# Biases on GpSimd, evenly cut q and k work, spread v and w_out loads, and an odd PV distance in a fused attention and feed-forward kernel

## The chip, the cores and the metric

The kernel runs on one core of one Trainium2 chip. The metric is the device time of one execution in microseconds (us), taken on that core. Executions of one kernel mostly lie within about 1% of each other, and chips differ a little; so every kernel was run beside the kernel before on the same chip, and ratios are taken against those runs. An execution is called slow if it lies over 1.5% above the fastest of its kernel, and slow ones are left out of ratios.

## The reference

Thresholded attention over 8 batches of 8 heads (576 rows, head size 64), followed by a feed-forward block over all 4,608 rows (512 to 2,048, leaky ReLU, back to 512).

```python
scores = scale * np.matmul(q, k.transpose(0, 1, 3, 2))
thresh = np.max(scores, axis=-1, keepdims=True) - tau
scores = np.where(scores >= thresh, scores, -1000000000.0)
scores = scores - np.max(scores, axis=-1, keepdims=True)
attn = np.exp(scores)
attn = attn / (np.sum(attn, axis=-1, keepdims=True) + 1e-09)
x = np.matmul(attn, v)            # heads are then laid side by side
h = x @ w_in
out = np.maximum(0.01 * h, h) @ w_out
```

## The kernel before

The program is a hand-ordered software pipeline of 144 steps. A step takes one block of 128 query rows for two heads, and a batch has 18 steps. In the first two batches PV takes one block at a time, later mostly two. In the text, "step 43" is the pass of the loop below with s = 43. Engines run their own instructions in exactly this order. The feed-forward block is worked off beside it in units: an h unit makes a piece of the hidden layer (hp, then gT), an o unit a part of the output (op, then osb).

```python
# one pass of the step loop (cut)
scores(s, sc)                                   # TensorE: sc = q k^T, three fp16 products
sa, sB = smax(0, sc, mx), smax(1, sc, mx)       # VectorE: sf = C * sc, and its row maximum; the two "sf"
bb = sb.tile([128, 2], FP32, tag="bb", ...)
nc.vector.tensor_scalar(out=bb, in0=mx, scalar1=-1.0, scalar2=tau_f, op0=AX.mult, op1=AX.add)
nc.scalar.activation(out=P_[:, 1, :], in_=sB, func=AF.Identity, bias=bb[:, 1:2], scale=1.0)
nc.gpsimd.tensor_scalar(out=P_[:, 0, :], in0=sa, scalar1=1.0, scalar2=bb[:, 0:1], ...)   # from step 4 on
leak()                                          # VectorE: gT = 0.01 * hp + gT
for f in (h, o): ...                            # ScalarE: gT = relu; VectorE: osb = op (output copy)
evacs = [pv(ui) for ui in pv_at.get(s, [])]     # TensorE: P V, LAG steps after its scores
if now is not None:
    nc.vector.reciprocal(out=rc, in_=usm[now])  # 1 / row sum
    nc.vector.tensor_scalar(out=W_[..., 1152:1280], in0=rc (broadcast), ...)             # "w copy"
    nc.sync.dma_start(out=uwt[now], in_=W_, transpose=True)                              # wt
# the clamp: int16 max on the bits of fp16
anchor[0] = nc.vector.tensor_scalar(out=pi, in0=pi, scalar1=NEG, scalar2=None, op0=AX.max)
for h in range(2):
    nc.scalar.activation(out=uW[ui][:, i, ds(576*h, 576)], in_=P_[:, h, :], func=AF.Exp, accum_out=...)
for f in evacs: f()                             # VectorE: xT = pv * (1 / row sum)
for t in ptick.get(s, []): t()                  # GpSimd: q and k work, ordered behind the clamp
for t in tick.get(s, []): t()                   # loads, transposes, ScalarE casts
```

The work for the next batch is hung on the steps of this one. q and k are loaded, split into an fp16 high and low part (ScalarE casts `hi`; GpSimd scales, `x64`, and subtracts, `lo`) and transposed by DMA (`turn`) into `kst` and `qst`:

```python
for b in range(1, B):
    s0 = 18 * (b - 1)
    for hb in range(2):
        t0 = s0 + PREP + (5 if b >= NARROW else 3) * hb       # PREP = 6
        if b == 1:
            t0 += 2
        at(t0 - 4, lambda b=b, hb=hb: load_half(k, kms, "km", b, hb))    # SyncE's queue, 576 KB
        at(t0 - 3, lambda b=b, hb=hb: load_half(q, qms, "qm", b, hb))
        at(t0 - 1, lambda b=b, hb=hb: hi("k", b, hb))
        at(t0 + 2, lambda b=b, hb=hb: hi("q", b, hb))
        ...                                                   # x64, lo and turn, six steps
    for i in range(4):
        at(max(s0 + 10, 12) + i, lambda b=b, i=i: load_v(b, i))          # GpSimd's queue
for g in range(8):
    at(WOUT + g // 2, lambda g=g: load_w_out(g))              # WOUT = 1: two of 256 KB in a step
```

## Time and profile before

| | us |
|---|---|
| Device time, first three runs | 546.72 median (546.09 to 549.38) |
| Span of the profiled run | 546.5 |
| Start, up to step 43 | 170.0 |
| Steps 43 to 133 (five batches of 18 steps) | 300.2, 60.0 per batch |
| Steps 133 to 143 | 33.4 |
| Tail after step 143 | 42.9 |

A step is counted from its R, the start of VectorE's second accumulator read in it, as in the prediction below.

Busy time by stretch, for the middle and for steps 6 to 12 (columns: stretch, us, then busy us and instructions of TensorE, its weight loads, VectorE, ScalarE and GpSimd, granted clock, that is the share of TensorE's full clock that it was given, DMA share, GB/s):

```profile
170.03:470.24 300.21, 277.79 (x2916) 171.38 (x2914) 293.75 (x823) 255.42 (x566) 160.93 (x209) 0.99 1.10 204
35.30:59.36 24.06, 18.01 (x183) 11.35 (x182) 16.45 (x56) 16.56 (x38) 10.86 (x14) 0.59 1.09 244
```

VectorE is busy 293.75 of 300.21 us in the middle, and the DMA share is 1.10 (over 1, so the records of packets overlap). Both look full. The waits of the middle (columns: us in total, times, longest us) seem to settle it for VectorE:

```profile
PE pv L367 <- DMA wt<-w: 1.6, 2, 1.3
DVE sf L396 <- PE sc L336: 1.5, 3, 0.8
```

TensorE waited for a transposed wt for 1.6 us in five batches, and VectorE for scores for 1.5. Nobody waits for a transfer worth speaking of.

### The profile page before, as it was taken

How to read it: one execution, taken by the hardware profiler on the slowest of the kernel's cores; microseconds unless marked ns; L12 is line 12 of the kernel's file. 1: busy time of each engine (PE TensorE's matmuls, PEld its weight loads, DVE VectorE, ACT ScalarE, POOL GpSimd, SP SyncE). 2: the span in 40 equal slices, each digit the busy share in tenths (PEclk: the TensorE clock that was granted, in tenths of full speed). 3: DMA queues.
4: the chain of work that ended last, by engine and by line, in shares of the span. 5: the costliest groups of instructions: out<-in, count | busy, mean ns of one | idle time of the engine just before them, and what ended most of it. 6: DMA issues, size and time to landing. Idle time of an engine off the chain costs nothing. (4 is left out here: it accounts for less than half of the span.)

```text
span 546.5 us, 14352 instructions
## 1 busy us (share of the span) xinstructions
PE 484.4 (89%) x5328; PEld 305.0 (56%) x5328; DVE 491.3 (90%) x1385; ACT 423.4 (77%) x922; POOL 253.2 (46%) x338
## 2 busy tenths in 40 slices
PE   5558987989999888988989899999999899999996
PEld 4325654656666555555555555555565565666663
DVE  5766997999999999999999999999999999999542
ACT  5657875888888888898788888898888888888430
POOL 5344761268425772468325852477335842222000
PEclk9655998999999989999999999999999999999999
DMA  8999999999999999999999999999999999667401
GB/s 215 192 161 288 163 169 175 203 222 199 181 184 208 241 191 164 217 242 180 189 197 256 194 174 175 234 239 190 188 219 247 203 195 182 129 134 125 109 24 58
DMA packets 280133, 101.85 MB, mean 186 GB/s; under 512 B 254976, under 2 KB 267264, under 8 KB 280064
## 3 DMA queue, kind: packets, MB, share of 16 engines
q1 hardware_dynamic: 267008, 92.03, 87.4%
q0 software_dynamic: 13056, 8.92, 12.8%
q8 instruction: 41, 0.67, 0.5%
q14 instruction: 28, 0.23, 0.2%
HBM read 36.70 MB, written 9.44 MB: 84 GB/s over the span
## 5 line engine op out<-in xcount | busy, mean ns | idle before, releaser
L559 ACT ACTIVATE w<-P 128x576 f16<-128x576 f16 x288 | 193.9, 674 | 34.5 <-DVE P L554 25.5
L396 DVE TENSOR_SCALAR_CACHE_REDUCE sf<-sc 128x576 f32<-128x576 f32 x288 | 204.7, 746 | 11.0 <-PE sc L336 10.9
L525 POOL TENSOR_SCALAR P<-sf,bb 128x576 f16<-128x576 f32 x140 | 107.8, 770 | 196.9 <-DVE bb L523 179.6
L336 PE MATMUL sc<-kst,qst 64*128 64x320 f16 (+1 forms) x1536 | 142.2, 298 | 30.5 <-DVE sf L396 23.7
L241 PE MATMUL hp<-xT,win 128*128 128x128 f16 (+1 forms) x1600 | 153.8, 244 | 2.9 <-DVE xT L377 2.7
L241 PE MATMUL op<-wout,gT 128*128 128x512 f16 x576 | 149.1, 382 | 7.8 <-DVE osb L277 4.6
L524 ACT ACTIVATE P<-sf,bb 128x576 f16<-128x576 f32 x144 | 111.2, 772 | 56.3 <-DVE bb L523 53.5
L241 PEld LDWEIGHTS <-win 128*128 128x128 f16 x1600 | 124.0, 99 | 45.1 <-issue 7.9
L336 PEld LDWEIGHTS <-qst 64*128 64x128 f16 x1536 | 77.6, 97 | 81.0 <-issue 54.3
L223 DVE SCALAR_TENSOR_TENSOR gT<-hp,gT 128x512 f16<-128x512 f32 x144 | 98.4, 683 | 12.7 <-ACT gT L255 12.7
L255 ACT ACTIVATE gT<-hp 128x512 f16<-128x512 f32 x144 | 83.3, 579 | 19.0 <-PE hp L241 19.0
L241 PEld LDWEIGHTS <-gT 128*128 128x128 f16 x576 | 46.6, 98 | 70.4 <-issue 25.1
L554 DVE TENSOR_SCALAR P<-P 128x1152 int16<-128x1152 int16 x144 | 82.9, 576 | 0.0
L367 PE MATMUL pv<-wt,v 128*64 128x256 f16 (+2 forms) x1160 | 59.1, 240 | 8.0 <-DMA wt<-w 7.3
L367 PEld LDWEIGHTS <-v 128*64 128x64 f16 x1160 | 40.4, 112 | 25.4 <-issue 14.5
L559 ACT ACTIVATION_READ_ACCUMULATOR w<-P 128x1 f32 x288 | 53.8, 187 | 0.0
L159 POOL TENSOR_TENSOR ks<-km,ks 128x320 f16<-128x320 f32 (+1 forms) x56 | 40.8, 748 | 6.0 <-DVE P L554 4.8
L159 POOL TENSOR_TENSOR qs<-qm,qs 128x576 f16<-128x576 f32 x28 | 35.8, 1278 | 16.5 <-DVE P L554 12.7
L544 DVE TENSOR_SCALAR w<-rc 128x256 f16<-128x256 f32 (+1 forms) x92 | 36.5, 396 | 3.2
L523 DVE TENSOR_SCALAR bb<-mx 128x2 f32<-128x2 f32 x144 | 34.2, 238 | 5.0
L377 DVE TENSOR_TENSOR xT<-pv,wt 128x128 f16<-128x128 f32 x128 | 33.3, 292 | 2.5 <-PE pv L367 2.4
L277 DVE COPY osb<-op 128x512 f32<-128x512 f32 x36 | 24.5, 680 | 4.1 <-PE op L241 4.1
(33 smaller groups left out, 210.3 us busy)
## 6 DMA issues: line engine op xcount, KB each, us to landing
km<-in_k_dram SPq DMA_DIRECT2D x16, 576.0 KB, 4.8
qm<-in_q_dram SPq DMA_DIRECT2D x16, 576.0 KB, 5.0
out_dram<-osb SPq DMA_DIRECT2D x36, 256.0 KB, 3.8
v<-in_v_dram POOLq DMA_DIRECT2D x16, 160.0 KB, 5.0
v<-in_v_dram POOLq DMA_DIRECT2D x16, 128.0 KB, 5.0
win<-in_moe_w_in_dram POOLq DMA_DIRECT2D x8, 256.0 KB, 9.6
wout<-in_moe_w_out_dram POOLq DMA_DIRECT2D x8, 256.0 KB, 9.1
wt<-w SPq DMA_TRANSPOSE x92, 5.6
```

The lines of the kernel that those rows point to most:

```text
L159: return nc.gpsimd.tensor_tensor(out=dst[:, h], in0=src[:, h], in1=h_[:, h], op=AX.subtract)
L223: nc.vector.scalar_tensor_tensor(out=G.g[u], in0=hp, scalar=0.01, in1=G.g[u], op0=AX.mult, op1=AX.add)
L241: nc.tensor.matmul(out=out_, lhsT=lhsT, rhs=rhs, start=start, stop=stop, skip_group_check=True)
L255: nc.scalar.activation(out=G.g[u], in_=hp, func=AF.Relu, bias=0.0, scale=0.99)
L336: nc.tensor.matmul(out=sc[h][:, cols], lhsT=qt[r, g, qi, ds(2 * c, 2), :].rearrange("p t r -> p (t r)"), rhs=rhs, start=(i == 0), stop=(i ...
L367: nc.tensor.matmul(out=o_[ds(64 * h, 64)], lhsT=vt[:, pp, h, j, :], rhs=w_[:, :, 4 * h + j, :], start=(j == 0), stop=(j == 4), skip_group_ ...
L396: nc.vector.tensor_scalar(out=sf, in0=sc[h][:, ds(SC0, 576)], scalar1=C, scalar2=None, op0=AX.mult, op1=AX.max, accum_out=mx[:, h : h + 1])
L524: nc.scalar.activation(out=P_[:, 1, :], in_=sB, func=AF.Identity, bias=bb[:, 1:2], scale=1.0)
L525: (nc.vector if s < SPOOL else nc.gpsimd).tensor_scalar(out=P_[:, 0, :], in0=sa, scalar1=1.0, scalar2=bb[:, 0:1], op0=AX.mult, op1=AX.add)
L544: nc.vector.tensor_scalar(out=W_[:, :, 1152:1280].rearrange("p i (h r) -> p i h r", h=2), in0=rc[:, 0:nw, :].unsqueeze(3).to_broadcast([12 ...
L554: anchor[0] = nc.vector.tensor_scalar(out=pi, in0=pi, scalar1=NEG, scalar2=None, op0=AX.max)
L559: nc.scalar.activation(out=uW[ui][:, i, ds(576 * h, 576)], in_=P_[:, h, :], func=AF.Exp, bias=exp_bias, scale=1.0, accum_out=usm[ui][:, i, ...
```

## The change

The intent is to relieve VectorE: the two-column bias bb goes to GpSimd. PV runs seven steps behind its scores instead of six (an odd distance), so that the two xT evictions leave the steps that hold rc and w. GpSimd's q and k work is cut into seven even pieces in place of uneven ones over six steps, begins earlier, and no longer shares steps with the loads of v, which move to the steps after a batch's start. The w_out loads go one to a step over eight steps instead of two to a step over four. In the tail every second output copy goes to ScalarE, and the o units' endings are placed before the h units'.

```diff
-    LAG = 6
+    LAG = 7
-    PREP = 6
+    PREP = (4, 10)
+    PREP1 = (5, 10)
-    OSB_ACT = False
+    LAGN = 6
-    WOUT = 1
+    WOUT = 2
@@ osb_act
-        return OSB_ACT
+        osbs[0] += 1
+        return tail[0] and osbs[0] % 2 == 0
@@ q and k work
-            t0 = s0 + PREP + (5 if b >= NARROW else 3) * hb
-            if b == 1:
-                t0 += 2
+            t0 = s0 + (PREP1 if b < 2 else PREP)[hb]
             at(t0 - 4, ... load_half(k, kms, "km", b, hb))
             at(t0 - 3, ... load_half(q, qms, "qm", b, hb))
             at(t0 - 1, ... hi("k", b, hb))
-            at(t0 + 2, ... hi("q", b, hb))
+            at(t0 + 1, ... hi("q", b, hb))
+            for i, what in enumerate(("k0x", "k0l", "k1x q0x", "k1l", "q0l", "q1x", "q1l")):
+                ...                      # x: x64, l: lo; piece i in step t0 + i
+            at(t0 + 4, ... turn("k", b, hb))
+            for g in range(2):
+                at(t0 + 7 + g, ... turn("q", b, hb, g))
         for i in range(4):
-            at(max(s0 + 10, 12) + i, lambda b=b, i=i: load_v(b, i))
+            at(18 * b + i, lambda b=b, i=i: load_v(b, i))
     for g in range(8):
-        at(WOUT + g // 2, lambda g=g: load_w_out(g))
+        at(WOUT + g, lambda g=g: load_w_out(g))
@@ distance of PV
-        lag = LAG if last < ENDS else LAGE
+        lag = LAGN if units[ui][0] < NARROW else LAG if last < ENDS else LAGE
@@ step loop
-            nc.vector.tensor_scalar(out=bb, in0=mx, ...)
+            (nc.vector if s < SPOOL else nc.gpsimd).tensor_scalar(out=bb, in0=mx, ...)
-            for f in (h, o):
+            for f in (o, h):
```

More of the change, by code (lines that the diff above doesn't have):

```diff
@@ L55 @@
     BONUS = 0.0
-    OSB_ACT = False
+    LAGN = 6
     LAGE = 4
     ENDS = 130
-    WOUT = 1
-    PT = 0
+    WOUT = 2
     SPOOL = 4
@@ L235 @@
     tail = [False]
+    osbs = [0]
     def osb_act():
-        return OSB_ACT
+        osbs[0] += 1
+        return tail[0] and osbs[0] % 2 == 0
     def mm(out_, lhsT, rhs, start, stop):
@@ L468 @@
             at(t0 - 1, lambda b=b, hb=hb: hi("k", b, hb))
-            at(t0 + 2, lambda b=b, hb=hb: hi("q", b, hb))
-            i = 0
-            for nm in "kq":
-                for h in range(2):
-                    at(t0 + i + PT, lambda nm=nm, h=h, b=b, hb=hb: after_anchor(x64(nm, b, hb, h)), ptick)
-                    def f(nm=nm, h=h, b=b, hb=hb):
-                        for part in PARTS[nm]:
-                            after_anchor(lo(nm, b, hb, h, part))
-                    at(t0 + i + (h if nm == "k" else 1) + PT, f, ptick)
-                    i += 1 + h
-                for g in ([None] if nm == "k" else range(2)):
-                    at(t0 + i + (g or 0), lambda nm=nm, b=b, hb=hb, g=g: turn(nm, b, hb, g))
+            at(t0 + 1, lambda b=b, hb=hb: hi("q", b, hb))
+            for i, what in enumerate(("k0x", "k0l", "k1x q0x", "k1l", "q0l", "q1x", "q1l")):
+                for w in what.split():
+                    nm, h = w[0], int(w[1])
+                    if w[2] == "x":
+                        at(t0 + i, lambda nm=nm, h=h, b=b, hb=hb: after_anchor(x64(nm, b, hb, h)), ptick)
+                    else:
+                        for part in PARTS[nm]:
+                            at(t0 + i, lambda nm=nm, h=h, b=b, hb=hb, part=part: after_anchor(lo(nm, b, hb, h, part)), ptick)
+            at(t0 + 4, lambda b=b, hb=hb: turn("k", b, hb))
+            for g in range(2):
+                at(t0 + 7 + g, lambda b=b, hb=hb, g=g: turn("q", b, hb, g))
         for i in range(4):
-            at(max(s0 + 10, 12) + i, lambda b=b, i=i: load_v(b, i))
+            at(18 * b + i, lambda b=b, i=i: load_v(b, i))
     for g in range(8):
-        at(WOUT + g // 2, lambda g=g: load_w_out(g))
+        at(WOUT + g, lambda g=g: load_w_out(g))
     pv_at = {}
@@ L522 @@
             bb = sb.tile([128, 2], FP32, tag="bb", bufs=4, name="bb")
-            nc.vector.tensor_scalar(out=bb, in0=mx, scalar1=-1.0, scalar2=tau_f, op0=AX.mult, op1=AX.add)
+            (nc.vector if s < SPOOL else nc.gpsimd).tensor_scalar(out=bb, in0=mx, scalar1=-1.0, scalar2=tau_f, op0=AX.mult, op1=AX.add)
             nc.scalar.activation(out=P_[:, 1, :], in_=sB, func=AF.Identity, bias=bb[:, 1:2], scale=1.0)
```

## The prediction

> **What bounds the kernel now.** First I read the page's busy shares and slices. Three engines look close to full, so the page alone does not decide.
>
> ```profile
> PE 484.4 (89%) x5328; PEld 305.0 (56%) x5328; DVE 491.3 (90%) x1385; ACT 423.4 (77%) x922; POOL 253.2 (46%) x338
> DVE  5766997999999999999999999999999999999542
> PEclk9655998999999989999999999999999999999999
> ```
>
> The reader is to see that VectorE is full from slice 7 to 37, and that there is a start (0 to 95 us, with idle time) and a tail (from 504 us, TensorE alone). Next I read busy time by stretches. In four steps without q or k work VectorE is busy 12.69 of 12.90 us:
>
> ```profile
> 327.69:340.59 12.90, 12.52 (x116) 7.59 (x116) 12.69 (x38) 10.64 (x24) 2.98 (x4) 1.00 1.06 168
> 504.00:546.50 42.50, 36.10 (x353) 23.39 (x352) 18.69 (x37) 13.44 (x26) 0.74 (x1) 1.00 0.25 66
> ```
>
> So VectorE sets the pace in the middle. But its busy time contains waiting, which only the timeline shows. One light step, and the head of the next, heavy one:
>
> ```profile
> 213.52 0.08 DVE L396 DVE_READ_ACCUMULATOR sf<-sc 128x1 f32 x1
> 213.63 0.17 DVE L523 TENSOR_SCALAR bb<-mx 128x2 f32<-128x2 f32 x1
> 213.71 0.68 DVE L223 SCALAR_TENSOR_TENSOR gT<-hp,gT 128x512 f16<-128x512 f32 x1
> ...
> 214.00 0.75 POOL L525 TENSOR_SCALAR P<-sf,bb 128x576 f16<-128x576 f32 x1 [2.65 <-DVE bb L523]
> 214.31 0.75 DVE L554 TENSOR_SCALAR P<-P 128x1152 int16<-128x1152 int16 x1
> ...
> 214.98 0.74 DVE L396 TENSOR_SCALAR_CACHE_REDUCE sf<-sc 128x576 f32<-128x576 f32 x1
> ```
>
> The columns are start, duration, engine, line. I count from R, the start of the step's second accumulator read (here 213.52). bb stands at R+0.11, gT at R+0.19, the int16 clamp (L554) at R+0.79. The clamp takes 0.45 us in steps where nothing is in its way; here it takes 0.75, and ends 0.31 after GpSimd's P (214.00 to 214.75, that is R+0.48 to R+1.23). So **GpSimd's P, not VectorE's own work, decides when a light step goes on**. The w copy (L544) of the heavy steps ends late in the same way: 0.38 instead of 0.29. In q/k steps bb itself is caught behind GpSimd:
>
> ```profile
> 309.60 0.75 POOL L525 TENSOR_SCALAR P<-sf,bb 128x576 f16<-128x576 f32 x1
> ...
> 309.80 0.62 DVE L523 TENSOR_SCALAR bb<-mx 128x2 f32<-128x2 f32 x1
> ```
>
> The clean steps repeat in fours: light 2.81, heavy (rc, w, two xT) 3.40, light 2.81, heavy with the output copy osb 3.91; 12.93 us together. From R of step 43 (170.03) to R of step 133 (470.24) five batches of 18 steps take 60.04 us each; 18 clean steps would take 18 x 12.93 / 4 = 58.2.
>
> **What the Trainium skill says.** "SBUF — State Buffer", section "Who interferes with whom": VectorE and GpSimd share one pair of SBUF ports under an exclusive lock held for a whole instruction; tensor_scalar without accumulator output may take it, an instruction with at most one SBUF input and outside those modes does not. The trace agrees: bb, w and the clamp are stretched under GpSimd's P, while gT (one input in PSUM) keeps 0.68 us. "GPSIMD Engine Reference", section 3.1: about 1.03 cycles per element at 1.2 GHz for simple bodies. I use it to split GpSimd's 576-column scaling (km, 0.67 us here) into 0.49 of stream and about 0.18 fixed: my estimate for a two-column bb there. The trace has no such instruction; its shortest GpSimd record is a 128x1 memset of 0.11. "Trainium Kernel Development and Optimization", section "Performance Expectations": matmul busy time is a bad metric since matmuls are pipelined. So I take TensorE's load from start to start below.
>
> **The change part by part.**
>
> 1. *bb to GpSimd* (140 of 144). VectorE loses 0.17 + waits: gT can start at R instead of R+0.19. GpSimd's chain: the read ends R+0.08, plus 0.10 from engine to engine (bb end to P start where P has one wait), bb about 0.18, 0.08 from GpSimd to itself (km end to ks start in this trace), so P runs from R+0.44 to R+1.19. Before it ended at R+1.23 in clean steps: there P had two waits, and the order of instructions shows that the separate wait stood on VectorE, which cost 0.20 from bb's end instead of 0.10; afterwards only the wait on ScalarE is separate, and it is long fulfilled. So the lock is released **hardly earlier (0.04)**, and VectorE's 0.19 is only worth something where VectorE has lock-free work to put before R+1.19.
>
> 2. *PV seven steps behind.* The order of VectorE's instructions shows what the title doesn't say: with an odd distance the two xT leave the step with rc and w, and, more important, **osb goes from the rc/w step into the xT step**. Steps after, with start-to-start costs from the trace (gT 0.60, osb 0.60, rc 0.20, clamp 0.37 unblocked, xT pair 0.40, the two sf 1.35):
>    - gT, rc, w, clamp: w is at 0.81, blocked until 1.19, ends so that the clamp starts 0.07 after the release (as before) at 1.26; sf at 1.63; step 2.98.
>    - gT, clamp, xT: clamp blocked until 1.19, next instruction 0.24 later (as before), xT 0.40, sf 1.35: 3.18.
>    - gT, osb, clamp, xT: clamp at 1.21, free; 1.58, 1.98, 3.33.
>    Four steps: 2.98 x 2 + 3.18 + 3.33 = 12.47 instead of 12.93, that is 56.1 per 18. The osb now fills a wait; before it came on top.
>
> 3. *Seven even pieces, v apart.* Before, 60.04 - 58.2 = 1.8 us per batch went to q/k steps (bb of 0.62, clamps of 0.98). After, a piece runs from the clamp's end to the next bb. Behind rc/w steps this is about 1.35 us, and the four k pieces there (ks pair, 1.42) overrun by 0.1 to 0.3; behind xT steps it is about 1.75, enough for 1.28 and 1.34. About 0.8 per batch, plus 0.5 for ScalarE, whose q/k casts (1.2 us each) now stand in odd steps, just ahead of a row sum that rc wants. So 57.4 per batch: (60.04 - 57.4) x 5 = **13 us**.
>
> 4. *The start.* Step 7 lasts 7.71 us against 2.93 for its neighbours: rc waits 5.2 for ScalarE, which waits 5.7 for a transpose (wt) running beside eight w_out loads issued in four steps. Spread over eight steps: 3 saved (0 to 5 possible). Steps 18 and 19 stand 2.4 and 1.5 us because TensorE waits for the transposed q of batch 1; its first half now starts three steps earlier: 2.5. Steps 9 to 16 and 25 to 34 exceed their clean length by 5.9 and 3.0 us, mostly the lock (a bb of 1.60); half of it, 4.5. The lighter VectorE in clean narrow steps: 2. Together **12 us**.
>
> 5. *End.* Steps 134 to 143: 1. Tail: half of the osb on ScalarE removes some of TensorE's waits (three of 0.25, one of 0.78), but one h unit more is left for it (one more step without gT before it), 0.9: nothing. The exchanged order of the o and h endings moves only copies within a step: nothing.
>
> Sum 13 + 12 + 1 = 26, so 520.7. I keep two or three of them back for friction I have not seen: 523.5.
>
> **Rivals.**
>
> - *GpSimd's chain becomes the bound.* If bb there takes 0.25 and the wait behind it 0.15, P ends at 1.33 to 1.35: steps of 3.13, 3.34, 3.13, 3.34, together 12.94, and the middle gains nothing but the q/k part. Then 537 to 541. For it: all hangs on a duration that this trace has not. Against it: 0.11 and 0.18 above. Each 0.05 on P's end is about 6 us in all.
> - *TensorE takes over.* From start to start: sc 0.84, op 0.88, hp 0.97, and 0.67 of pv every other step: 12.10 per four steps, 97% of 12.47. It would cap the middle at about 54.5 per batch, so it does not bind at my figure, but any wait of TensorE costs then. In the trace it waits for sf 24 us in all and lags by up to 0.4 after a pv, which the two-step rhythm takes back. If it binds, 525 to 530.
> - *Transfers.* wt transposes take 5.6 us to landing (median); PV has a step more for it, and TensorE waited for wt only 7.3 us in five places. Hidden in the middle; in the start the loads may only shift the stall, making (4) worth 5: 530.
> - *Everything of bb is gained* (0.19 x 140 = 27 us from that alone), if the lock were no limit: 505 to 510. The stretched clamps speak against it.
>
> **Range and chances.** 523.5, with 512 to 538 from 6 us either way on P's end, and 3 to 17 for the start. Under 535.8 is faster by over 2%: the first rival, or a start that gives nothing together with TensorE, would be needed to miss it: 0.83. Within 2% 0.15. Slower 0.02: nothing is added to VectorE.
>
> **What would show it.** GpSimd's bb of 0.15 to 0.21 us, P ending at about R+1.19; clean steps alternating 2.98 and 3.18 or 3.33; clamps still at about 0.85 us in xT steps without osb, and 0.45 with it; 18 steps in 57 to 58 us; step 7 near 3 to 5 us; no waits for q in steps 18 and 19. Wrong would be: P at R+1.3 or later, TensorE waiting for nothing while VectorE waits for sc, or a tail longer than 44 us.

## More of the kernel before

From the page: the slices of the DMA engines (tenths of the mean busy share of the 16 engines), and two queues with packets, MB and the share of 16 engines' span that their packets took.

```profile
DMA  8999999999999999999999999999999999667401
...
q1 hardware_dynamic: 267008, 92.03, 87.4%
q0 software_dynamic: 13056, 8.92, 12.8%
```

The reader is to see that the transfers are at nine tenths or more from the second slice to the 34th, at a mean of only 186 GB/s, and that SyncE's queue q1 alone takes 87.4% of all engines' time.

## The result and the profile after

The changed kernel took 554.86 us in the median of four runs (553.41, 554.76, 554.95, and one slow at 564.78); the kernel before, in the same rounds, 547.73 (546.09 to 549.38). The ratio of fast runs is 1.0121, with a 95% interval of 1.0073 to 1.0169. Here and below a ratio is the mean time of one kernel's fast runs over that of the other's of the same rounds, so it is not quite the ratio of the quoted medians. The interval says that it is about 1.2% slower. The prediction was 523.5 and faster, with a range of 512 to 538. It missed the time by 31 us.

From the page of the changed kernel (for the groups: instruction, form, count, then busy us and mean ns of one, then idle us before them and what ended it):

```profile
PE 479.7 (87%) x5328; PEld 302.8 (55%) x5328; DVE 460.0 (83%) x1243; ACT 423.2 (77%) x924; POOL 281.0 (51%) x478
...
DVE  5873595899998999799969999599969998999542
...
DMA  9999999999999999999999999999999999976411
...
q1 hardware_dynamic: 267008, 92.03, 90.5%
q0 software_dynamic: 13056, 8.92, 13.5%
...
L523 POOL TENSOR_SCALAR bb<-mx 128x2 f32<-128x2 f32 x140 | 26.8, 191 | 105.0 <-DVE sf L398 98.7
...
L554 DVE TENSOR_SCALAR P<-P 128x1152 int16<-128x1152 int16 x144 | 74.8, 519 | 0.0
```

VectorE lost 31 us of busy time (491.3 to 460.0, and 142 instructions), as was intended, and the span did not shrink. The row of VectorE's slices, full from slice 8 to 37 before (the prediction says 7, but its line has a 7 there), now has holes of 5, 6 and 7. The DMA row, also full before, is full still: the same 101.85 MB in the same packets, now over 104.0% of the engines' span instead of 100.2% (the two queues added). Busy time by stretch, same columns as before, for the same three parts of the program (the middle; steps 6 to 12; the tail):

```profile
175.38:474.16 298.78, 275.13 (x2905) 169.96 (x2903) 273.55 (x731) 252.78 (x564) 177.56 (x296) 0.97 1.13 203
35.00:65.80 30.80, 15.90 (x157) 9.29 (x157) 14.62 (x50) 14.80 (x32) 16.70 (x27) 0.61 1.33 158
507.20:551.60 44.40, 37.95 (x372) 24.55 (x366) 18.42 (x38) 15.27 (x30) 0.94 (x2) 0.99 0.27 69
```

In the middle VectorE's busy time falls by 20.2 us and the stretch by 1.4: the freed time became idle time. The rate of the transfers, 204 GB/s before, is 203 now. Steps 6 to 12 take 6.7 us longer; while they run, the DMA share is at 1.33 and the rate at 158 GB/s instead of 244. The tail is 1.5 us longer.

The waits of the middle of the changed kernel (columns as before):

```profile
ACT ks L149 <- DMA km<-in_k_dram: 17.7, 4, 5.3
PE sc L338 <- DMA qst<-qs: 11.9, 5, 4.3
DVE sf L398 <- PE sc L338: 10.0, 10, 3.8
...
PE pv L369 <- DMA wt<-w: 3.8, 3, 3.2
```

Where before nobody waited for a transfer, ScalarE's cast of k now waits for its load, TensorE's scores for the transposed q, PV for wt, and behind them VectorE for scores. One such place, step 75, in the order of time (start, duration, engine, line, what, and in brackets the idle time and what ended it):

```profile
274.15 3.85 SPq L179 DMA_TRANSPOSE qst<-qs  x2
...
278.05 1.34 SPq L96 DMA_DIRECT2D km<-in_k_dram  x1
278.07 0.63 POOL L121 DMA_DIRECT2D v<-in_v_dram  x1 [0.81 <-DVE P L554]
...
279.91 1.62 PE L338 MATMUL sc<-kst,qst 64*128 64x320 f16 x12 [4.26 <-DMA qst<-qs]
...
281.57 0.76 DVE L398 TENSOR_SCALAR_CACHE_REDUCE sf<-sc 128x576 f32<-128x576 f32 x1 [3.79 <-PE sc L338]
```

TensorE stands 4.26 us for qst and VectorE 3.79 us for the scores, while a k load and a v load are being issued on two queues. The transposes of q were late already when they were issued: GpSimd had finished the last piece of q at 263.06, but SyncE, which works off its transfer instructions one after the other, reached them at 274.15, with its earlier ones standing almost end to end from 261.80 on. But where no transfer is late, the steps run as planned. A clean step, R = 214.18:

```profile
214.18 0.68 DVE L223 SCALAR_TENSOR_TENSOR gT<-hp,gT 128x512 f16<-128x512 f32 x1
...
214.35 0.19 POOL L523 TENSOR_SCALAR bb<-mx 128x2 f32<-128x2 f32 x1 [0.52 <-DVE sf L398]
...
214.64 0.75 POOL L525 TENSOR_SCALAR P<-sf,bb 128x576 f16<-128x576 f32 x1
...
214.78 0.92 DVE L554 TENSOR_SCALAR P<-P 128x1152 int16<-128x1152 int16 x1
```

GpSimd's bb takes 0.19 us, its P ends at 215.39, that is R+1.21, and VectorE's clamp, which starts at 214.78, is held until then and lasts 0.92. In a step with the output copy the same clamp takes 0.44, since osb stands in its place while GpSimd works:

```profile
327.68 0.68 DVE L223 SCALAR_TENSOR_TENSOR gT<-hp,gT 128x512 f16<-128x512 f32 x1
...
328.13 0.75 POOL L525 TENSOR_SCALAR P<-sf,bb 128x576 f16<-128x576 f32 x1
...
328.28 0.67 DVE L279 COPY osb<-op 128x512 f32<-128x512 f32 x1
...
328.88 0.44 DVE L554 TENSOR_SCALAR P<-P 128x1152 int16<-128x1152 int16 x1
```

Clean steps of the changed kernel last 2.99, 3.18 and 3.31 us; the prediction had 2.98, 3.18 and 3.33. So its model of VectorE was right, and something that it did not count took the gain.

### The profile page after: what moved, and what is told of

Its sections match the earlier page's. It is cut to its first block, busy times and chain, and to the rows that moved or that the text cites.

```text
span 551.6 us, 14363 instructions
## 1 busy us (share of the span) xinstructions
PE 479.7 (87%) x5328; PEld 302.8 (55%) x5328; DVE 460.0 (83%) x1243; ACT 423.2 (77%) x924; POOL 281.0 (51%) x478
## 2 busy tenths in 40 slices
DMA packets 280133, 101.85 MB, mean 185 GB/s; under 512 B 254976, under 2 KB 267264, under 8 KB 280064
## 4 chain that ended last, share of the span: by engine, by line
DVE 37%; PE 18%; DMA 16%; issue 14%; ACT 7%; POOL 4%; SPq 2%; POOLq 0%; DVEq 0%; ACTq 0%
DVE sf L398 15%; DMA wt<-w 9%; PE op L243 7%; DVE P L554 6%; DVE gT L223 6%; PE hp L243 5%; DMA km<-in_k_dram 4%; DVE w L544 4%; PE sc L338 4%; ACT w L559 4%; POOL P L525 2%; DVE osb L279 2%; DVE xT L379 2%; SPq L179 2%; DMA qm<-in_q_dram 2%
## 5 line engine op out<-in xcount | busy, mean ns | idle before, releaser
L338 PE MATMUL sc<-kst,qst 64*128 64x320 f16 (+1 forms) x1536 | 134.7, 300 | 32.6 <-DMA qst<-qs 18.4
L243 PE MATMUL op<-wout,gT 128*128 128x512 f16 x576 | 152.8, 390 | 2.8 <-DVE osb L279 2.3
L338 PEld LDWEIGHTS <-qst 64*128 64x128 f16 x1536 | 73.8, 98 | 78.6 <-issue 34.1
L525 POOL TENSOR_SCALAR P<-sf,bb 128x576 f16<-128x576 f32 x140 | 109.4, 781 | 14.2
L369 PE MATMUL pv<-wt,v 128*64 128x256 f16 (+2 forms) x1160 | 60.1, 243 | 23.4 <-DMA wt<-w 22.7
L523 POOL TENSOR_SCALAR bb<-mx 128x2 f32<-128x2 f32 x140 | 26.8, 191 | 105.0 <-DVE sf L398 98.7
L554 DVE TENSOR_SCALAR P<-P 128x1152 int16<-128x1152 int16 x144 | 74.8, 519 | 0.0
L544 DVE TENSOR_SCALAR w<-rc 128x256 f16<-128x256 f32 (+1 forms) x92 | 41.1, 446 | 3.3
L149 ACT ACTIVATE ks<-km 128x640 f16<-128x640 f32 (+1 forms) x32 | 20.0, 671 | 22.0 <-DMA km<-in_k_dram 22.0
```

Source lines behind the costliest of these rows:

```text
L243: nc.tensor.matmul(out=out_, lhsT=lhsT, rhs=rhs, start=start, stop=stop, skip_group_check=True)
L338: nc.tensor.matmul(out=sc[h][:, cols], lhsT=qt[r, g, qi, ds(2 * c, 2), :].rearrange("p t r -> p (t r)"), rhs=rhs, start=(i == 0), stop=(i ...
L369: nc.tensor.matmul(out=o_[ds(64 * h, 64)], lhsT=vt[:, pp, h, j, :], rhs=w_[:, :, 4 * h + j, :], start=(j == 0), stop=(j == 4), skip_group_ ...
L525: (nc.vector if s < SPOOL else nc.gpsimd).tensor_scalar(out=P_[:, 0, :], in0=sa, scalar1=1.0, scalar2=bb[:, 0:1], op0=AX.mult, op1=AX.add)
L544: nc.vector.tensor_scalar(out=W_[:, :, 1152:1280].rearrange("p i (h r) -> p i h r", h=2), in0=rc[:, 0:nw, :].unsqueeze(3).to_broadcast([12 ...
```

## The experiments

The theory after the result: the 16 DMA engines were already nearly as full as VectorE, so that a faster VectorE only runs into the transfers; and in the start the spread w_out loads now compete with the wt transposes of more steps. The rivals: one of the changed placements (v loads, q and k work) is what delays the transfers, and could be put back; SyncE's queue, in which all transposes, q and k loads and stores stand in one order, is the limit, not the engines behind it; or GpSimd's chain delays things. All kernels gave the right result, except c3 and d1. Their outputs are wrong, which doesn't matter for the times. In the numbers, "start" is the time up to step 43, "middle" the five batches from there to step 133, both from the profiled run, one for each kernel, so that differences of a us or two between middles may be chance.

| kernel | start | middle | tail | median us | ratio to before (95%) |
|---|---|---|---|---|---|
| before | 170.0 | 300.2 | 42.9 | 547.73 | 1 |
| changed | 175.4 | 298.8 | 44.4 | 554.86 | 1.0121 (1.0073 to 1.0169) |
| a1: biases and lag only | 164.4 | 299.4 | 44.4 | 541.30 | 0.9875 (0.9801 to 0.9948) |
| a2: changed, v loads back | 176.6 | 298.5 | 44.3 | 554.30 | 1.0098 (1.0031 to 1.0165) |
| a3: changed, q/k places back | 173.1 | 301.8 | 44.4 | 554.38 | 1.0091 (1.0026 to 1.0156) |
| a4: changed, start back | 175.0 | 301.7 | 44.4 | 552.73 | 1.0061 (0.9988 to 1.0134) |
| b5: before + biases | 164.7 | 296.9 | 42.9 | 542.99 | 0.9906 (0.9829 to 0.9983) |
| b6: before + lag | 168.7 | 300.8 | 45.0 | 549.73 | 1.0012 (0.9951 to 1.0074) |
| c1: a1, loads on another queue | 176.8 | 305.3 | 44.9 | 564.91 | 1.0271 (1.0181 to 1.0361) |
| c3: a1 without v | 163.8 | 285.2 | 44.4 | 531.98 | 0.9680 (0.9607 to 0.9753) |
| d1: changed without v | 174.3 | 285.8 | 44.2 | 538.98 | 0.9889 (0.9813 to 0.9965) |
| d4: changed, w_out back | 167.8 | 296.4 | 44.3 | 544.68 | 0.9910 (0.9880 to 0.9941) |
| x1: before, a k load twice | 170.5 | 317.5 | 42.6 | 564.48 | 1.0327 (1.0272 to 1.0383) |
| e1: a1 with bonus | 165.9 | 306.1 | 39.1 | 550.36 | 1.0055 (1.0029 to 1.0080) |

### a1: only the biases, the lag and the order of endings

```diff
 # against the kernel before
-    LAG = 6
+    LAG = 7; LAGN = 6
-            nc.vector.tensor_scalar(out=bb, ...)
+            (nc.vector if s < SPOOL else nc.gpsimd).tensor_scalar(out=bb, ...)
-            for f in (h, o):
+            for f in (o, h):
 # and every second output copy of the tail on ScalarE; loads, q/k work and w_out stay
```

> The changed kernel with the transfers and the q/k work put back where the kernel before has them (k/q loads, pieces, turns, v loads, w_out loads); left of the change are the biases on GpSimd, PV seven steps behind, and the small end parts. Theory 'placement': the 5 to 7 us stalls at steps 57, 75, 95, 111 (three steps into a batch) come from q turns, k/q loads and v loads of the new schedule standing together there, and those of steps 8 to 11 and 19 from the spread w_out loads and the earlier loads of batch 1. Then this kernel keeps the faster clean steps (2.98, 3.18, 3.31), loses the stalls, and takes 525 to 537 us; batches in 57.0 to 58.5 us. Rival 'capacity': the DMA queues can't serve a batch in less than about 59.7 us whatever the order; then the batches stay at 59.3 to 60 and the whole at 543 to 548. Rival 'biases': GpSimd's biases delay ScalarE's half and cost time themselves; then 550 or more.

It took 541.30 us against 549.23, ratio 0.9875, which lies between the ranges of its theories. So the parts that move VectorE's work are worth about 1.2% (the interval excludes 1), and the parts that move transfers and GpSimd's pieces cost about 2.5% on top (1.0121 over 0.9875). The gain came in the start (5.6 us, of which 2.6 in steps 6 to 12); the middle, 59.9 per batch, gained as little as in the changed kernel. Its batches show another obstacle, though: long steps 49, 67, 85 and 103 of 5.4 to 6.0 us, of which the timeline shows the cause. At step 49:

```profile
181.57 1.42 POOL L159 TENSOR_TENSOR ks<-km,ks 128x320 f16<-128x320 f32 x2
...
182.93 0.66 POOL L121 DMA_DIRECT2D v<-in_v_dram  x1
...
183.66 0.19 POOL L525 TENSOR_SCALAR bb<-mx 128x2 f32<-128x2 f32 x1
```

VectorE's read ended at 182.71, but bb stands behind k work and the issue of a v load on GpSimd, and starts 0.95 later. Giving GpSimd the bias makes the bias wait for GpSimd's other work, where that is cut as before; the even pieces of the changed kernel remove these steps. So a1 alone does not tell which of the two holds its middle.

### a2: the v loads back

```diff
-            at(18 * b + i, lambda b=b, i=i: load_v(b, i))
+            at(max(s0 + 10, 12) + i, lambda b=b, i=i: load_v(b, i))
```

> The changed kernel with only the v loads put back (steps 10 to 13 of the batch before, not the first four steps of their own). If v beside the k/q loads is what stalls the batch starts, 4 to 5 us per batch in five batches go: 532 to 538, steps 57, 75, 95, 111 near 3.0 to 3.5. If it is the k/q loads behind the q turns on the one queue that is worked in order, v matters little: 550 to 556. Capacity: 550 to 556.

554.30 us, start 176.6, middle 298.5: nothing changed within what runs scatter. Where the v loads stand is not the cause.

### a3: the q and k work nearer to its old places

```diff
-    PREP = (4, 10)
+    PREP = (6, 11)
```

> The changed kernel with the k/q loads and their work of batches 2 to 7 moved back by two steps (first half) and one step (second half), v left in the first four steps of its batch. If the k load standing right behind the two q turns of the half before, with ScalarE's cast due three steps later, is the cause: 530 to 540, waits of ScalarE's k cast for its load down from 22 us to under 5. If v's loads are the cause: the stalls stay, 550 to 558. Capacity: no change over 5 us.

554.38 us, middle 301.8. The wait of ScalarE for k loads over the whole run fell from 22.0 to 4.8 us, but TensorE's wait for qst rose from 18.4 to 26.6. The stall only moved from one transfer to another, as one would expect if the sum of the transfers is the limit and not the place of one of them.

### a4: the start back

```diff
-    PREP1 = (5, 10)
+    PREP1 = (8, 11)
-    WOUT = 2
+    WOUT = 1
-        at(WOUT + g, lambda g=g: load_w_out(g))
+        at(WOUT + g // 2, lambda g=g: load_w_out(g))
```

> The changed kernel with w_out issued as before (two a step from step 1) and batch 1's loads and q/k work as before (steps 8 and 11). If the new placing of these is what made the first 43 steps 5.4 us longer than before instead of 12 us shorter: 540 to 546, step 19 (10.35 us) near 5, step 43 reached at 163 to 168 us instead of 175. If the start is lost to something else (the biases, the faster steps meeting the same transfers): 551 to 557.

Steps 6 to 12 came back from 30.8 to 23.6 us, but steps 18 to 24 went from 27.3 to 33.5, since both halves of q were now turned one step later than in the kernel before (t0 + 7 where it has t0 + 6): steps 18 and 20 lasted 9.6 and 9.8 us, with TensorE waiting 5.8 and 5.9 us in them for qst. The start as a whole is where it was. This run undid two things and misplaced one, so it is inconclusive for the start; d4 was made to replace it.

### b5 and b6: one part of a1 each

```diff
 # b5, against the kernel before
-            nc.vector.tensor_scalar(out=bb, ...)
+            (nc.vector if s < SPOOL else nc.gpsimd).tensor_scalar(out=bb, ...)
 # b6, against the kernel before
-    LAG = 6
+    LAG = 7; LAGN = 6
```

> The kernel before with one part of the change: both biases on GpSimd, PV still six steps behind. By the prediction's arithmetic, with P ending at R+1.20: light steps 2.78 to 2.80 (2.81 before), rc/w/xT steps 3.38 (3.40), with osb 3.73 (3.91), 12.7 per four steps instead of 12.93, a batch of 18 in 57.1 clean. If the transfers hold a batch at 59.8 us, the middle moves under 2 us and only the start may gain: 543 to 548. If VectorE is the bound in the middle: 536 to 541.

> The kernel before with one part of the change: PV seven steps behind for batches 2 to 7, biases on VectorE. Clean steps 3.00, 3.20, 3.00, 3.50, together 12.7; osb partly fills the wait for the lock. Same alternatives: middle held by transfers, 544 to 550; VectorE the bound: 538 to 542.

The biases alone (b5): 542.99 against 549.47, ratio 0.9906, start 164.7. The lag alone (b6): 1.0012, no effect on the middle and a tail of 45.0 instead of 42.9. So all of a1's gain that is certain is the biases', and most of it is in the start (b5's own time lies between its two ranges). The odd lag, which by the model saves VectorE's wait in every step with osb, gained nothing measurable by itself beside these transfers, and lengthens the tail by about 2 us.

### c1: is it SyncE's queue?

```diff
 # against a1: loads of q and k of batches 1 to 7, and all output stores, on ScalarE's queue
-        nc.sync.dma_start(out=m, ...)
+        (nc.scalar if b else nc.sync).dma_start(out=m, ...)
-            return lambda: nc.sync.dma_start(out=G.rows[i], in_=osb)
+            return lambda: nc.scalar.dma_start(out=G.rows[i], in_=osb)
```

> Run a1 with the k/q loads of batches 1 to 7 and the output stores issued from ScalarE instead of SyncE, so that the queue that SyncE works in order holds transposes alone. Theory 'one queue': SyncE's transfer instructions take 95% of the middle in a1, of that some 6 us a batch for loads and stores; taken off, batches fall to VectorE's 57 to 58 us, the whole to 528 to 536, and the waits for q and wt shrink. Theory 'engines': the 16 DMA engines themselves are full; then the batches stay at 59 to 61 and the whole at 538 to 545. A third outcome, ScalarE delayed by issuing (8 issues a batch at about 0.6 us): batches over 60.

564.91 us, ratio 1.0271. The time covered by SyncE's transfer instructions fell to 0.84 to 0.91 of the middle's batches (in a1 0.93 to 0.96), so its queue was relieved; yet the middle got longer, 61.1 per batch, and PV waited longer for wt (all of the run, columns as before):

```profile
PE pv L369 <- DMA wt<-w: 24.6, 6, 9.2
```

The Trainium skill says in "Trainium Kernel Development and Optimization", section "Key Constraints", that transfers issued from SyncE, ScalarE and GpSimd run on the same 16 engines and interleave, so that a second issuing engine saves issue time only. This run agrees: a relieved queue, 0.87 instead of 0.95, and no gain. By the batches (over 60) the outcome is the third one expected, ScalarE delayed by its issues of 0.37 to 0.66 us; but the trace does not show that delay: in the middle VectorE waited for ScalarE's gT and row sums 8.6 and 7.3 us, in a1 8.6 and 8.0, while PV's wait for wt rose from 0.8 to 8.3 us. The wt transpose that PV waited for in step 96 had only transposes before it on SyncE's queue, and yet took 16.0 us to landing, beside a k and a q load on the other one. So the queue alone is not the limit; c1 does not show that it has no part.

### c3 and d1: no v loads after the second batch (result wrong)

```diff
 # c3 against a1, d1 against the changed kernel
-        after_anchor(nc.gpsimd.dma_start(out=out_, in_=in_))
+        if b < 2:
+            after_anchor(nc.gpsimd.dma_start(out=out_, in_=in_))
```

> Run a1 without the v loads of batches 2 to 7 (results wrong on purpose, v of batches 0 and 1 is used again). They come from GpSimd's queue, not SyncE's, and are some 4 us a batch of the engines' time by their shortest packets. Theory 'engines': batches fall by 2 to 4 us, the whole to 526 to 535. Theory 'one queue' (SyncE's order and issue): batches fall by under 1.5 us, the whole 535 to 542.

> The changed kernel without the v loads of batches 2 to 7 (results wrong on purpose). Its v loads stand in steps without q/k work of GpSimd, so unlike in c3 nothing but the transfer itself, and 0.65 us of GpSimd's idle time, goes. Theory 'engines': the DMA engines are the bound of the middle; five batches fall from 298.8 us to 283 to 290 (57.0 to 58.0 each, VectorE's length), the stalls three steps into a batch nearly vanish, the whole 533 to 543 with the slow start unchanged. Rival 'GpSimd': in c3 it was GpSimd's backlog, not the transfers, that went; then five batches stay at 295 to 300 and the whole at 549 to 556.

c3 took 531.98, with a middle of 57.0 per batch. Taken alone it is ambiguous: in a1 the issue of v stands in GpSimd's backlog, and the long steps 49, 67 and 85 shrank to 4.3 to 4.7 with it. d1 does the same to the changed kernel, where v is not beside q and k work on GpSimd:

```profile
174.27:460.10 285.83, 270.82 (x2901) 168.36 (x2899) 272.66 (x733) 253.06 (x564) 164.91 (x276) 0.99 1.10 204
```

VectorE's busy time is as in the changed kernel (272.66 and 273.55), the rate of the transfers still is 204 GB/s, but the stretch is 13.0 us shorter: 57.15 us per batch, where the prediction had 57.4. The waits of the middle shrink with it: VectorE's for scores from 10.0 to 1.4, TensorE's for qst from 11.9 to 5.1, ScalarE's for k from 17.7 to 8.4. Taking 0.59 of 12.1 MB per batch from the transfers gives back what the change was to gain. What d1 itself does not separate is GpSimd's issuing time, four times 0.63 us per batch and so as long as the gain. The trace of the changed kernel does: after each of the 20 v issues of the middle GpSimd stood idle for 0.5 us or more before the next bias, which began 0.16 or 0.17 us after R, as in clean steps. So the issues delayed nothing, and what d1 took away is the transfers. The two traces also show how the v loads act on SyncE's queue, on which v never stood: SyncE's transfer instructions cover 0.94 to 0.96 of the batches in d1 too, but its wt transposes are shorter, 3.76 us in the mean instead of 4.06.

### x1: more transfers in the kernel before

```diff
 # against the kernel before: each k load of batches 2 to 7 a second time, into a tile that nobody reads
+        if nm == "km" and b >= 2:
+            m2 = sb.tile([128, 2, 576], FP32, tag="km2", bufs=1, name="km2")
+            nc.sync.dma_start(out=m2, in_=...)
```

> The kernel before with each k load of batches 2 to 7 issued a second time, into a tile that nobody reads (12 more transfers of 576 KB; by their shortest packets 1.5 us of the engines each, about 3 us a batch; SyncE's issue 0.6 us each). If the DMA engines already share the bound in the kernel before: five batches from 300.2 to 308 to 316, the whole 556 to 564. If the kernel before has room for them (VectorE the bound with 60 us, transfers hidden): under 3 us in all, 549 to 553.

```profile
170.49:488.01 317.52, 281.24 (x2916) 173.10 (x2916) 295.06 (x823) 255.75 (x567) 161.27 (x209) 0.97 1.13 212
```

564.48 us, ratio 1.0327: 17.3 us more in the five batches, 3.5 per batch, a little over the range expected. In the middle PV's wait for wt rose from 1.6 to 20.4 us. No engine but SyncE got any work. Estimated from the shortest packets (93 ns for 2,304 bytes) the added packets are 3 us of the engines' time per batch. So even the kernel before, in whose middle nobody waited for transfers, had no room for two more loads in a batch: its two limits, VectorE and the transfers, must have lain close together. (The run adds to SyncE's queue as well as to the engines; c1 and d1 speak on which of them it is.)

### d4: only the w_out loads back

```diff
 # against the changed kernel
-    WOUT = 2
+    WOUT = 1
-        at(WOUT + g, lambda g=g: load_w_out(g))
+        at(WOUT + g // 2, lambda g=g: load_w_out(g))
```

> The changed kernel with only the w_out loads as before (two a step from step 1). If spreading them is what stretched steps 6 to 12 from 24.1 to 30.8 us: that segment at 23 to 25 us, the stall of step 19 perhaps smaller, the whole 543 to 549. If it was the earlier loads and q/k work of batch 1: 29 to 31 us, the whole 551 to 556.

The start went from 175.4 to 167.8, steps 6 to 12 from 30.8 to 24.6 us. Over 20 runs the median was 544.68 (537.13 to 556.92) against 547.12 of the kernel before; the ratio of fast runs is 0.991. Nine of the 20 runs lie over 1.5% above the fastest and count as slow, so that this ratio favours d4; that of the medians of all runs is 0.9955. Against the changed kernel's 1.0121 either is 1.7 to 2.1%. Two queries of transfers, from 24 to 66 us (what, queue, count, KB, median us from issue to landing), first of the changed kernel, then of d4:

```profile
wout<-in_moe_w_out_dram POOLq DMA_DIRECT2D x8, 256.0 KB, 11.3
...
wt<-w SPq DMA_TRANSPOSE x8, 12.4
```

```profile
wout<-in_moe_w_out_dram POOLq DMA_DIRECT2D x6, 256.0 KB, 10.0
...
wt<-w SPq DMA_TRANSPOSE x12, 5.1
```

In the median a wt transpose takes 12.4 us to landing while w_out loads are in flight in every step, and 5.1 in d4, where they are done sooner. In d4 too the first three, issued among the w_out loads, took 9.3 to 15.1, and the later ones 3.5 to 6.5. The packets show it as well: in steps 6 to 12 a 256-byte packet of the transposes took 39.3 ns in the mean in the changed kernel, 22.7 in d4. Every kernel fits: the four with spread loads (changed, a2, a3, d1) take 30.7 to 32.5 us for steps 6 to 12; nine with the old placing (before, a1, a4, b5, b6, c3, d4, x1, e1) take 20.8 to 24.6; c1, with q and k loads on another queue, 27.6.

### e1: a feed-forward unit more now and then, to shorten the tail

```diff
 # against a1
-    BONUS = 0.0
+    BONUS = 0.15
```

> Run a1 with a bonus of 0.15 unit a step while more than eight h and o units wait: 5 more units are done in the middle, 3 fewer h units are left to the end (16 instead of 19 gT). If the middle is bound by the transfers, TensorE and VectorE have room for them there: the tail 44.5 falls to 38 to 40, five batches stay at 299 to 302, the whole 535 to 539. If the middle is bound by VectorE, the units cost there what they save at the end: 540 to 543.

A miss: the tail fell from 44.4 to 39.1, but the middle rose from 299.4 to 306.1 and steps 133 to 143 from 32.4 to 37.5. Ratio 1.0055. The work of the tail costs more in the middle than at the end. So a1's middle had no room for it, against what was expected from the theory (299 to 302 us). VectorE, or GpSimd's order in a1, may be close to its limit there too; which, no run tells.

Of all kernels with right results, a1 is the best, at 0.9875 of the kernel before and about 2.4% under the changed one; b5 and d4 are not to be told from it by their intervals.

## Why the prediction was wrong

The prediction's terms, against the profiled runs (spans 546.5 and 551.6). Of its own sum the prediction held back 2.8, and the medians of the times differ by 7.1 and not 5.1, so the miss of 31 us in the time agrees with the sum of the terms only to within such amounts (the table is rounded):

| term | predicted | measured | missing |
|---|---|---|---|
| parts 1 to 3, steps 43 to 133 | 13.2 shorter | 1.4 shorter | 11.8 |
| part 4, up to step 43 | 12 shorter | 5.4 longer | 17.4 |
| part 5, steps 133 to 143 | 1 shorter | 0.3 shorter | 0.7 |
| part 5, tail | 0 | 1.5 longer | 1.5 |
| sum | 26 shorter | 5.1 longer | 31.3 |

- **bb on GpSimd, right.** 0.18 was estimated and 0.19 measured; P was to end at R+1.19 and ends at R+1.20 to 1.22 in 54 of the 90 steps of the middle; "hardly earlier" was right. In the others, nearly all with k and q work, P ends by R+1.84, but once at R+3.61: in step 95 bb stood behind a k piece that waited, through ScalarE's cast, for a late k load. So the bias on GpSimd is also a new way for a late load to reach VectorE.
- **The odd distance, right in the step and worth nothing by itself.** The three step lengths hold to 0.02 us, osb fills the wait, and the clamp takes 0.92 without and 0.44 with it. The section of the skill on the shared ports that the prediction drew on held in these steps. But b6 shows no gain from the lag alone. One thing the model lacks: in nine steps of the middle with the same VectorE work as the step of 3.18, bb was delayed to R+0.31 to 0.33. There the clamp started before P, took 0.44 or 0.45 us instead of 0.91 or 0.92, and P had to wait and ended at R+1.66 or 1.67; eight of the nine steps lasted 2.72 to 2.79 us. So a later P can make the step shorter; what the delay costs further on, no run tells.
- **Seven even pieces, not shown to be worth anything.** In a1, with the old pieces, bb stands behind k work in some long steps, and the even pieces remove these. Without v the middle comes to 57.15 per batch in d1, as against 57.4 predicted; but c3, with the old pieces, comes to 57.0 as well. That d1 is so near to the prediction is in part chance: it still has five long steps in the middle (59, 76, 95, 97 and 113, of 4.2 to 5.1 us), and shorter ones of 2.72, as just described, that the model lacks.
- **The step that failed in the middle is the rival "Transfers":** "Hidden in the middle". It rested on 5.6 us to landing and on TensorE's waits for wt, which are waits under the pace of the kernel before. That a transfer isn't waited for does not mean that the engines have room for the same transfers in a shorter time. The middle moves the same bytes in any of these schedules, so a shorter batch needs a higher rate, and the rate did not rise: 204 before, 203 after, 204 in d1 with fewer bytes. (It is no fixed limit in GB/s: x1, with more of the long packets, moved 212, in longer batches.) x1 and d1 show it from both sides. Five batches were to take 287 and took 298.8: the term mis-sized is 59.8 for 57.4 per batch. The prediction also laid all of the 1.8 us per batch over clean steps on q and k work; how much of it was the transfers' is not known.
- **The step that failed in the start is part 4:** "Spread over eight steps: 3 saved". Before, the loads were a burst that hurt one step (step 7, 7.71 us); spread, they hurt steps 8 to 11 (5.6, 5.7, 4.8 and 7.9 us). d4 shows it to be 7.6 us of the start, and 6.2 in steps 6 to 12 alone. Of the rest, "no waits for q in steps 18 and 19" held for step 18 (5.5 us before, 3.0 after), which the first half's earlier start serves, and failed for step 19, which took 10.3 us (d4: 7.9) where it had 5.3. The prediction counted on the wrong half: the scores after step 19 need the second half of q, whose transposes stand in steps 17 and 18 before and after the change. The last piece of it was ready at 82.43 us, but SyncE, with its instructions end to end from 78.91, issued the transpose only at 90.81; TensorE waited 6.6 us, until 95.97. The lighter VectorE gave what was expected at the lock (4.5): in a1 and b5, with the old transfers, steps 9 to 16 and 25 to 34 are 4.3 and 3.9 us shorter. The clean narrow steps, of which 2 was expected, gave about 0.5; that a1 and b5 reach step 43 as much as 5.6 and 5.3 us earlier is also owed to step 7, whose wait for wt is 1.7 us shorter.
- **The tail,** "nothing", is 1.5 us longer: the lag of seven leaves one feed-forward unit more to it, 19 instead of 18. The prediction saw the unit (0.9) and set the ScalarE copies against it; b6, which has no such copies, has 45.0. A tail over 44 us, one of the prediction's own signs of being wrong, came true with 44.4.
- **The rivals "GpSimd's chain" and "TensorE takes over" did not occur** in the changed kernel: in clean steps P ends where it should, and the longest waits of TensorE and VectorE are for transfers or behind such waits. The granted clock of the changed run was lower (0.940 against 0.959), but d4's profiled run had 0.945 and was 10.8 us faster, so the clock does not explain the loss.

What stays open is what exactly limits the transfers. From the packet records of the middle of the changed kernel, the 256-byte packets of the transposes take 49.8 us of each engine's time per batch, at a mean of 24.8 ns, though half of all such packets take 18 ns. With every packet at the short end of its kind the engines would need some 49 us of a batch of 60; in d1, about 45 of 57. In the batches of before, changed, d1 and x1 this share is 0.78 to 0.86 (with the tenth percentile of each kind for its short end). In the middle of the changed kernel the 256-byte packets took 33.1 ns in the mean while packets of the v loads were in flight, and 24.3 otherwise; but why about four fifths is the ceiling no run tells, nor how large the part of SyncE's in-order queue is. That it has a part, the traces make likely: its instructions cover 0.95 to 0.96 of the changed kernel's batches, and it issued the transposes of q 8.8 us after their last piece was ready (mean of the last ten halves), against 5.6 before. But a full queue is not the cause by itself, since loads on another queue make its instructions longer (d1).

## What to carry to other kernels

Before counting on a faster engine, work out for each other resource the shortest time in which it could do the same work, the DMA engines too: a wait view shows only who is late at today's pace, and a resource without waiters can have no room left. The cheap test is to add work to the suspected resource alone (here one more load that nobody reads): if the time grows by about that work, it is at or near its limit. And where short transfers that others wait for share the engines with bulk loads, spreading the bulk can spread the delay instead of thinning it.

## What the Trainium skill lacked or had wrong

- "DMA: Bandwidth & Descriptors", section "Latency and other measured facts", gives transposes by DMA an effective 261 GB/s with a non-contiguous middle dimension, and 350 to 400 in the contiguous case. Here, beside loads and stores, the engines moved 203 to 212 GB/s in all in the middles of the kernel before, the changed one, d1 and x1, about two thirds of it by transposes, and one load more or less changed the time; at the usual 18 ns for a 256-byte packet, 16 engines would move 228 GB/s (an estimate from the records). The page has no figure for transposes in company, nor for what they suffer from bulk loads: a wt transpose landed after 5.1 us in the median with one placing of the w_out loads and after 12.4 with another.
- "Perfetto Trace Analysis", section "Roofline", measures memory use as all DMA throughput over a peak of 358 GB/s. The kernel before stood at 186, about half of that, and yet one more load per half batch made it 3.3% slower (x1). This number alone would have misled here, where most packets are of 256 bytes; the page does not stop at it, but asks further which DMA resource binds.
- "GPSIMD Engine Reference", section 3.1, has the rate per element but no cost of a very short instruction: a 128x2 tensor_scalar took 0.19 us.
- No page that I read says how a wait view can hide a second limit close under the first; here nobody waited for a transfer in the middle before (1.6 us in 300), and 13.0 us hung on the v loads in the changed kernel (d1).
